# Sixteen eight-row transfers of V in place of output weights on sixteen partitions, in a two-layer decode block

## The chip, the cores and the metric

The kernel runs on one core of one Trainium2 chip. The metric is the device time of one execution in microseconds (us). Before the change three runs took 2570.63, 2570.76 and 2570.87 us; the median is 2570.76 us. One execution was profiled; its span, from the first to the last instruction, is 2568.7 us.

## What is computed

Two tokens (batch 2, one position each, width 512) go twice through the same pair of layers: grouped-query attention over a cache of 32768 positions (32 query heads, 8 key/value heads, head size 128) and a gated feed-forward of width 1792. All is float32.

```python
def _A_ref(x, k_cache, v_cache, wq, wo):
    ...
    scores = jnp.einsum("bhqd,bhkd->bhqk", q, k) * (Dh ** -0.5)
    p = _softmax(scores, axis=-1)
    o = jnp.einsum("bhqk,bhkd->bhqd", p, v)
    return ... @ wo
def _B_ref(x, w_gate, w_up, w_down):
    ...
    h = _gelu(g) * u
    return jnp.einsum("bsf,fd->bsd", h, w_down)
x = x + _A_ref(_layernorm(x, axis=-1), ...)
x = x + _B_ref(_layernorm(x, axis=-1), ...)
x = x + _A_ref(_layernorm(x, axis=-1), ...)
x = x + _B_ref(_layernorm(x, axis=-1), ...)
```

Both attention layers read the same caches, so K and V of 16 pairs (key/value head, batch row) are read twice, 16 MB each for K and for V of a pair.

## The kernel before, in words

**Memory.** One tile `mem` of 128 partitions and 109 units takes all that comes from HBM; a unit is 512 floats (2 KB) in each partition. K or V of a pair has 64 units and normally comes as two pieces of 32 units (`CHUNK`), which is 8 MB a transfer. `take` (L150) finds a place for a piece: one of three spots of 32 units, or a fitting hole in what is left. `give` and `done` return a place when the last matmul that reads it has been written into the program.

**The stream.** `add` (L224) lists every transfer in the order in which it is to come: for each layer the query weights `wq`, then for each pair K and V, with the output weights `wo` of its head ahead of V's second piece, then gate/up (`gu`) and down (`wd`) weights. Layer 2 goes through the pairs backwards and still finds one pair's K and V of layer 1 in memory. `pump` (L183) issues the transfers in this order, each as soon as a place is free; all are issued by SyncE (SP), in order, on one queue. A transfer into a place that was used before waits in SP for the matmuls that read it and for the transfer that filled it.

**Completion semaphores.** Every transfer that a queue issues signals its landing on a semaphore. The built program has eight of them for transfers (DMAHW0 to DMAHW7), given out in turn. A transfer that gets a semaphore which an earlier transfer still holds has a wait for that earlier transfer's landing in front of it, unless SP has already waited for it.

**The work of a pair.** `scores` (L396) multiplies K's units with the queries on TensorE (PE) into the PSUM banks `S` (L414), VectorE (DVE) takes the maxima, `softmax` (L445) makes the weights, `values` (L473) multiplies V's units into the bank `A` (L485), and `combine` (L490) turns the result into `oT`. After the second batch row of a head `project` (L523) multiplies `oT` of its four query heads with the head's `wo` and adds into the bank `W`, which collects the layer's output. PE, DVE and ScalarE wait for the transfers; the program is written out by hand in this order (a manual schedule).

**Output weights on sixteen partitions.** For two of the sixteen (layer, head) combinations, head 6 in layer 1 and head 1 in layer 2 (`NARROW`, L63), part of the head's `wo` (2 and 3 of its four query heads) comes in another layout, `won`: 16 partitions instead of 128, as four transfers of four rows each (L193 to L197), in a whole spot of 32 units; the rest of that head's `wo` comes on 128 partitions as elsewhere. `narrow` (L505) then selects the matching rows of `oT` with eight small matmuls (L511), copies them (L514) and does 32 or 48 matmuls with 16 rows (L519) in place of 2 or 3 with 128 rows (L529).

Of the kernel before, what the change touches and what calls it, by code (L numbers as in the profile page):

```python
# [16 lines left out]
P = 128  # L17
NB = 2
HKV = 8
REP = 4  # L20
DM = 512
# [6 lines left out]
HALF = 2048  # L28
UNIT = 512
# [6 lines left out]
CHUNK = 32  # L36
# [23 lines left out]
WO_GROUPS = [[(0, 1), (2, 3), (4, 5), (6,), (7,)], [(7,), (6,), (5, 4), (3, 2), (1,), (0,)]]  # L60


NARROW = {(0, HKV - 2): 2, (1, 1): 3}  # L63
NROW = 16
NSEL = P // NROW


def pieces(split):

    out, s = [], 0  # L70
    for n in split:
        out.append((s, n))
        s += n
    return out
# [13 lines left out]
def plan():  # L88


    last, before = ORDER[-1], ORDER[-2]
    out = {}

    def put(kind, l, pair, spots):
        for (s, n), o in zip(parts(kind, l, pair), spots):
            out[kind, l, *pair, s] = o

    put("k", 0, before, [32, 0])
    put("v", 0, before, [64, 32])
    put("k", 0, last, [0, SPARE, 64])  # L100
    put("v", 0, last, [32, 16, 8, 4, 0])
    out["wo", 0, HKV - 1] = out["wo", 1, HKV - 1] = 105
    for i in range(8):
        out["gu", 0, i] = [94, 97.5, 101, 105][i % 4]
    for i in range(9):
        out["wd", 0, i] = out["wq", 1, i] = [94, 97, 101, 105][i % 4]
    put("k", 1, last, [96, 101, 105, 94, 64, 68, 72])
    put("k", 1, before, [85, 92, 64, 72, 32])
    put("v", 1, before, [0, 64])
    return out  # L110
# [22 lines left out]


@with_exitstack
def block_kernel(ctx: ExitStack, tc: tile.TileContext, x, consts, kt, vt, wq, wo, won, gu, wd, out):
    nc = tc.nc
    cp = ctx.enter_context(tc.tile_pool(name="cp", bufs=1))
    wk = ctx.enter_context(tc.tile_pool(name="wk", bufs=2))
# [4 lines left out]
    mem = cp.tile([P, UNITS * UNIT], F32, name="mem")  # L144
# [3 lines left out]
    planned = plan()  # L148

    def take(key, n):  # L150
        if key in planned:
            o = planned[key]
            if not any(s <= o and o + n <= e for s, e in holes):
                return None
        elif n == CHUNK:
            spots = [o for o in range(0, UNITS - CHUNK + 1, CHUNK)
                     if any(s <= o and o + n <= e for s, e in holes)]
            if not spots:
                return None
            o = spots[0]  # L160
        else:
            fit = [(e - s, -s, e) for s, e in holes if e - s >= n]
            if not fit:
                return None
            size, s, e = min(fit)
            o = -s
        for i, (s, e) in enumerate(holes):
            if s <= o and o + n <= e:
                holes[i:i + 1] = [(x, y) for x, y in ((s, o), (o + n, e)) if y > x]
                return o  # L170
        return None

    def give(o, n):
        holes.append((o, o + n))
        holes.sort()
        i = 0
        while i + 1 < len(holes):
            if holes[i][1] == holes[i + 1][0]:
                holes[i:i + 2] = [(holes[i][0], holes[i + 1][1])]
            else:  # L180
                i += 1

    def pump():  # L183
        while stream:
            key, src, rows, cols = stream[0]
            n = CHUNK if rows == NROW else cols / UNIT if key in planned else -(-cols // UNIT)
            o = take(key, n)
            if o is None:
                return
            stream.popleft()  # L190
            c = int(o * UNIT)
            at[key] = (o, n), mem[:rows, c:c + cols]
            if rows == NROW:  # L193


                for i in range(4):
                    nc.sync.dma_start(mem[i:NROW:4, c:c + cols], src[i])  # L197
            else:
                nc.sync.dma_start(at[key][1], src)

    def flat_of(key):
        if key not in at:
            pump()
        return at[key][1]

    def get(key, a):
        return flat_of(key).rearrange("p (a c) -> p a c", a=int(a))

    def done(key, s=0, n=None):

        o, size = at[key][0]
        n = size if n is None else n
        if s + n == size:
            del at[key]
        give(o + s, n)
        pump()
# [7 lines left out]
    def add(key, src, rows, cols):  # L224
        stream.append((key, src, rows, cols))
# [8 lines left out]
    for l in range(2):  # L234
        for i, (s, m) in enumerate(pieces(WQ_SPLIT[l])):
            add(("wq", l, i), wq[:, s * DM:(s + m) * DM], P, m * DM)
        for n, (g, b) in enumerate(orders[l]):
            second = meets(l, n)[1]
            vp = parts("v", l, (g, b))
            for s, m in parts("k", l, (g, b)):  # L240
                add(("k", l, g, b, s), flat(kt, g, b, s, m), P, m * UNIT)
            for s, m in [] if second else vp:
                if n % 2 == 1 and s == vp[1][0] and not meets(l, n)[0]:
                    group = wo_group(l, g)
                    o = g % 2 * HALF
                    if (l, g) in NARROW:
                        h = NARROW[l, g]
                        add(("won", l, g), won[l, :, :, :h * NSEL * DM], NROW, h * NSEL * DM)
                        add(("wo", l, g), wo[g // 2, :, o + h * DM:o + HALF], P, (REP - h) * DM)
                    elif len(group) == 2 and g == group[0]:  # L250
                        add(("wo", l, g), wo[g // 2], P, 2 * HALF)
                    elif len(group) == 1:
                        add(("wo", l, g), wo[g // 2, :, o:o + HALF], P, HALF)
                add(("v", l, g, b, s), flat(vt, g, b, s, m), P, m * UNIT)
            if meets(l, n)[0]:

                add(("wo", l, g), wo[g // 2, :, g % 2 * HALF:(g % 2 + 1) * HALF], P, HALF)
        for e in range(2):
            half_of = gu[e * P * FH:(e + 1) * P * FH].rearrange("(p c) -> p c", p=P)
            for j, (c, m) in enumerate(pieces(GU_SPLIT[l])):  # L260
                add(("gu", l, len(GU_SPLIT[l]) * e + j), half_of[:, c:c + m], P, m)
        for j, (o, m) in enumerate(pieces(WD_SPLIT[l])):
            add(("wd", l, j), wd[:, o * DM:(o + m) * DM], P, m * DM)
# [18 lines left out]
    ident = cst[:, C_ID:C_ID + P]  # L282
# [5 lines left out]
    rows = ident.rearrange("p (c r) -> p c r", r=32)[:, :, :NB]  # L288
# [31 lines left out]
    W = ps.tile([P, 512], F32, name="W")  # L320
# [5 lines left out]
    def big():  # L326
        return wk.tile([P, 512], F32, name="big")[:, :]
# [9 lines left out]
    def small():  # L337

        u = 0 if state["full"] else state["next"]
        state["next"] = 1 - u  # L340
        return M[u]
# [160 lines left out]
        diag = bass.AP(tensor=mt.tensor, offset=mt.offset, ap=[mt.ap[0], [1, REP], [P + REP, 4], [32, 4]])  # L502
        nc.vector.tensor_reduce(oT[:, :, b], diag, axis=AX.XY, op=OP.add)  # L503

    def narrow(l, g, oT, final):  # L505

        m = small()
        heads = NARROW[l, g]
        n = heads * NB
        for j in range(NSEL):  # L510
            nc.tensor.matmul(m[:NROW, n * j:n * j + n], ident[:, NROW * j:NROW * j + NROW],  # L511
                             oT[:, :heads, :].rearrange("p t b -> p (t b)"), start=True, stop=True)
        on = big()[:NROW, :NSEL * n]
        nc.vector.tensor_copy(on, m[:NROW, :NSEL * n])  # L514
        w = get(("won", l, g), NSEL * heads)
        for i in range(NSEL * heads):
            q = i % 4
            j, t = i % NSEL, i // NSEL
            nc.tensor.matmul(W[32 * q:32 * q + NB, :], on[:, n * j + NB * t:n * j + NB * t + NB], w[:, i, :],  # L519
                             start=False, stop=(final and q < heads and i + 4 >= NSEL * heads))  # L520
        done(("won", l, g))

    def project(l, g, oT, first, final):  # L523
        if (l, g) in NARROW:
            narrow(l, g, oT, final)
            h = NARROW[l, g]
            w = get(("wo", l, g), REP - h)
            for t in range(h, REP):
                nc.tensor.matmul(W[32 * t:32 * t + NB, :], oT[:, t, :], w[:, t - h, :], start=False, stop=final)  # L529
            done(("wo", l, g))  # L530
            return
        group = wo_group(l, g)
        key = "wo", l, group[0]
        w = get(key, REP * len(group))
        o = REP * (g - min(group))
        for t in range(REP):
            nc.tensor.matmul(W[32 * t:32 * t + NB, :], oT[:, t, :], w[:, o + t, :], start=first, stop=final)  # L537
        if g == group[-1]:
            done(key)
# [127 lines left out]
    for l in range(2):  # L667
        queries(l)
        stage(l, 0)
        for n, (g, b) in enumerate(orders[l]):  # L670
            if n % 2 == 0:
                oT = tiny("oT")
            p, linv = softmax(*scores(l, n, g, b))
# [16 lines left out]
    assert not stream  # L690


_INS = ["x", "consts", "kt", "vt", "wq", "wo", "won", "gu", "wd"]


def groups(x):
# [50 lines left out]
```

## Time and profile before

| what | value |
|---|---|
| median of 3 runs | 2570.76 us (2570.63 to 2570.87) |
| profiled execution, span | 2568.7 us |
| read from HBM | 1103.45 MB, 430 GB/s over the span |
| busy PE / DVE / ScalarE (ACT) / GpSimd (POOL) | 54% / 6% / 3% / 0% of the span |
| transfers by SP of V and of K at full size | 60 and 59, median 48.9 and 49.0 us from issue to landing |

The page of the profile gives, engine by engine, busy time and share of the span, then the span in 40 slices with the busy share in tenths, the clock that PE was granted, the share of time in which the 16 DMA engines were busy, and the rate. A row of a timeline gives start, duration, engine, line, operation, output and inputs, how often (x), and in brackets how long the engine had been idle before it and what ended that. "SPq" is SP's queue of issues; its duration is the issue alone, not the transfer. A row that merges several issues gives the time from the first to the end of the last.

### The profile page before, as it was taken

Reading aid. Unit: us, or ns where it says so; the run is one execution under the profiler, and the core shown is the slowest. Engines: PE = TensorE matmul, PEld = TensorE weight load, DVE = VectorE, ACT = ScalarE, POOL = GpSimd, SP = SyncE. Lnnn points to the kernel's source line nnn. Section 1 sums busy time; section 2 is a strip of 40 time slices with the busy share of each in tenths; the row PEclk is TensorE's granted clock in tenths of the full one; section 3 lists DMA queues with packets and bytes.
Section 4 is the critical chain, followed back from the end, with each engine's and each line's share of the span. In section 5 each row is a group of like instructions: output and inputs, shape, how many; then the busy total and the mean of one; then the engine's idle time right before and its main releaser. Section 6 shows DMA issues by size and latency. Waiting matters only on the chain.

```text
span 2568.7 us, 20340 instructions
## 1 busy us (share of the span) xinstructions
PE 1374.8 (54%) x9526; PEld 369.8 (14%) x9526; DVE 143.6 (6%) x483; ACT 81.4 (3%) x188; POOL 2.4 (0%) x8
## 2 busy tenths in 40 slices
PE   3545555545544554564686554454555544554657
PEld 1111111111111111111121111111111111111112
DVE  0000000000000000000011000000000000000001
ACT  0000000000000000000000000000000000000000
POOL 0000000000000000000000000000000000000000
PEclk8777777777777777777798677677776777777779
DMA  9999999999999999999999999999999999999998
GB/s 425 429 434 434 428 437 431 432 433 434 429 438 428 435 433 431 434 431 432 424 410 438 429 433 434 430 433 435 431 434 432 431 435 431 433 433 430 431 432 371
DMA packets 27507, 1104.81 MB, mean 430 GB/s; under 512 B 3200, under 2 KB 3456, under 8 KB 6912
## 3 DMA queue, kind: packets, MB, share of 16 engines
q1 hardware_dynamic: 27136, 1103.44, 99.6%
q8 instruction: 74, 1.21, 0.2%
q10 hardware_dynamic: 288, 0.08, 0.0%
q14 instruction: 9, 0.07, 0.0%
HBM read 1103.45 MB, written 0.07 MB: 430 GB/s over the span
## 4 chain that ended last, share of the span: by engine, by line
DMA 69%; PE 22%; another core or an unknown queue 8%; DVE 1%; issue 0%; ACT 0%; SPq 0%; POOL 0%; ACTq 0%; DVEq 0%
DMA mem<-in_vt 41%; DMA mem<-in_kt 24%; PE A L485 11%; PE S L414 9%; DMA aux<-in_consts 2%; DMA mem<-in_gu 1%; DMA mem<-in_wq 1%; DMA mem<-in_wd 0%; PE W L537 0%; PE M L498 0%; ACT big L494 0%; PE T L460 0%; PE W L519 0%; PE W L559 0%
## 5 line engine op out<-in xcount | busy, mean ns | idle before, releaser
L414 PE MATMUL S<-mem,aux 128*32 128x512 f32 x4032 | 575.5, 734 | 527.1 <-DMA mem<-in_kt 526.7
L485 PE MATMUL A<-mem,big 128*16 128x512 f32 x4096 | 584.7, 734 | 480.8 <-DMA mem<-in_vt 480.8
L414 PEld LDWEIGHTS S<-mem,aux 128*32 128x32 f32 x4032 | 144.9, 132 | 945.3 <-issue 508.2
L485 PEld LDWEIGHTS A<-mem,big 128*16 128x16 f32 x4096 | 122.6, 113 | 913.5 <-DMA mem<-in_vt 514.9
L417 DVE TENSOR_REDUCE aux<-S 128x1 f32<-128x512 f32 x63 | 43.6, 691 | 1110.1 <-PE S L414 1110.1
L457 ACT ACTIVATE big<-S,aux 128x512 f32<-128x512 f32 x63 | 42.7, 683 | 1187.1 <-DVE aux L453 1187.1
L460 PE MATMUL T<-aux,big 128*128 128x128 f32 x256 | 50.2, 342 | 39.0 <-ACT big L457 38.7
L503 DVE TENSOR_REDUCE aux<-M 128x4 f32<-128x64 f32 x32 | 7.2, 225 | 1103.4 <-PE M L498 1103.4
L494 ACT ACTIVATE big<-A,aux 128x512 f32<-128x512 f32 (+1 forms) x34 | 22.3, 661 | 1149.0 <-PE A L485 1149.0
L461 DVE COPY big<-T 128x512 f32<-128x512 f32 x64 | 43.8, 691 | 59.8 <-PE T L460 59.8
L460 PEld LDWEIGHTS T<-aux,big 128*128 128x128 f32 x256 | 35.8, 172 | 49.7 <-ACT big L457 49.5
L498 PE MATMUL M<-aux,big 128*128 128x128 f32 x128 | 21.3, 287 | 24.9 <-ACT big L494 24.9
L465 PE MATMUL M<-aux 128*128 128x4 f32 x64 | 17.2, 339 | 29.4 <-DVE aux L463 29.4
L449 PE MATMUL M<-aux 128*128 128x128 f32 x32 | 10.3, 323 | 34.5 <-DVE aux L447 34.5
L373 PE MATMUL M<-mem,aux 128*32 128x512 f32 x128 | 20.6, 690 | 4.4 <-DMA mem<-in_wq 3.9
L498 PEld LDWEIGHTS M<-aux,big 128*128 128x128 f32 x128 | 13.4, 140 | 53.2 <-ACT big L494 53.2
L465 PEld LDWEIGHTS M<-aux 128*128 128x128 f32 x64 | 14.4, 280 | 39.1 <-DVE aux L463 39.1
L537 PE MATMUL W<-mem,aux 128*2 128x512 f32 x96 | 12.5, 592 | 3.8 <-DVE aux L503 3.8
L333 PE MATMUL A<-aux 128*128 128x256 f32 (+2 forms) x42 | 14.3, 421 | 0.3 <-DVE aux L350 0.3
L449 PEld LDWEIGHTS M<-aux 128*128 128x128 f32 x32 | 4.2, 133 | 63.6 <-DVE aux L447 63.6
L359 PE MATMUL M<-aux 128*128 128x8 f32 x2 | 0.6, 356 | 23.2 <-DMA aux<-in_x 23.2
L457 ACT ACTIVATION_READ_ACCUMULATOR big<-S,aux 128x1 f32 x63 | 12.3, 196 | 0.0
(102 smaller groups left out, 188.8 us busy)
## 6 DMA issues: line engine op xcount, KB each, us to landing
mem<-in_gu SPq DMA_DIRECT2D x16, 896.0 KB, 24.5
mem<-in_wo SPq DMA_DIRECT2D x5, 2048.0 KB, 53.5
mem<-in_vt SPq DMA_DIRECT2D x2, 4096.0 KB, 42.2
mem<-in_kt SPq DMA_DIRECT2D x1, 7168.0 KB
mem<-in_wq SPq DMA_DIRECT2D x6, 1024.0 KB, 8.2
mem<-in_kt SPq DMA_DIRECT2D x1, 6144.0 KB
mem<-in_kt SPq DMA_DIRECT2D x5, 1024.0 KB, 8.7
mem<-in_kt SPq DMA_DIRECT2D x1, 4352.0 KB
```

The source lines that it names most:

```text
L333: nc.tensor.matmul(bank, ident[:, :bank.shape[0]], part.to_broadcast([P, n]), start=True, stop=True)
L373: nc.tensor.matmul(qp[32 * t:32 * t + 32, :], window(k, v), w[:, i - s, :], start=(i < 4), stop=(i >= 8 * KC - 4))
L414: nc.tensor.matmul(banks[u][32 * t:32 * t + 32, :], pad[:, PAD_Q - 4 * c:PAD_Q + 32 - 4 * c], w[:, j - s, :], start=(j == tile_of[0]), sto ...
L417: nc.vector.tensor_reduce(mx[:, u:u + 1], banks[u], axis=AX.X, op=OP.max)
L449: nc.tensor.transpose(m[:, :P], nm.to_broadcast([P, P]), ident)
L457: nc.scalar.activation(p[u], banks[u], AF.Exp, bias=bias, scale=SCALE, accum_out=ls[:, u:u + 1])
L460: nc.tensor.transpose(T[u][:, k * P:(k + 1) * P], p[u][:, k * P:(k + 1) * P], ident)
L461: nc.vector.tensor_copy(p[u], T[u])
L465: nc.tensor.matmul(m[:, :REP], both.to_broadcast([P, P]), same, start=True, stop=True)
L485: nc.tensor.matmul(A[32 * t:32 * t + 16, :], p[u][:, at_p:at_p + 16], w[:, QUAD * i + t, :], start=(j == 0), stop=(j == NU // QUAD - 1))
L494: nc.scalar.activation(md[:, i:i + 512 // n], A[:, i:i + 512 // n], AF.Copy, scale=linv)
L498: nc.tensor.transpose(m[:, c * P:(c + 1) * P], md[:, c * P:(c + 1) * P], ident)
```

## The change

No output weights come on 16 partitions any more: `NARROW`, `narrow` and the array `won` go, and the two heads project like all others, with `wo` of 4 units on 128 partitions (`wo_group` has them as groups of one). Instead two of V's pieces, the second piece of head 6, row 1, in layer 1, and the second piece of head 1, row 0, in layer 2, are split by units: the first 26 units come as one transfer of 128 rows, the last 6 units as sixteen transfers of eight rows each (12 KB a row, 96 KB a transfer). Transfer `i` takes rows `r, r+4, ... r+28` with `r = 32*(i//4) + i%4`.

```diff
-NARROW = {(0, HKV - 2): 2, (1, 1): 3}
-NROW = 16
-NSEL = P // NROW
+ASIDE = 6
+ASIDE_OF = {("v", 0, HKV - 2, 1, CHUNK), ("v", 1, 1, 0, CHUNK)}
...
-            n = CHUNK if rows == NROW else cols / UNIT if key in planned else -(-cols // UNIT)
+            n = cols / UNIT if key in planned else -(-cols // UNIT)
...
-            if rows == NROW:
-                for i in range(4):
-                    nc.sync.dma_start(mem[i:NROW:4, c:c + cols], src[i])
+            if key in ASIDE_OF:
+                m = cols - ASIDE * UNIT
+                nc.sync.dma_start(mem[:, c:c + m], src[:, :m])
+                for i in range(P // 8):
+                    r = 32 * (i // 4) + i % 4
+                    nc.sync.dma_start(mem[r:r + 29:4, c + m:c + cols], src[r:r + 29:4, m:])
...
-                    if (l, g) in NARROW:
-                        h = NARROW[l, g]
-                        add(("won", l, g), won[l, :, :, :h * NSEL * DM], NROW, h * NSEL * DM)
-                        add(("wo", l, g), wo[g // 2, :, o + h * DM:o + HALF], P, (REP - h) * DM)
-                    elif len(group) == 2 and g == group[0]:
+                    if len(group) == 2 and g == group[0]:
...
-    def narrow(l, g, oT, final):
-        m = small()
...
     def project(l, g, oT, first, final):
-        if (l, g) in NARROW:
-            narrow(l, g, oT, final)
...
-            return
         group = wo_group(l, g)
```

More of the change, by code (lines that the diff above doesn't have):

```diff
@@ L135, in block_kernel @@
 @with_exitstack
-def block_kernel(ctx: ExitStack, tc: tile.TileContext, x, consts, kt, vt, wq, wo, won, gu, wd, out):
+def block_kernel(ctx: ExitStack, tc: tile.TileContext, x, consts, kt, vt, wq, wo, gu, wd, out):
     nc = tc.nc
@@ L503, in combine @@
         nc.vector.tensor_reduce(oT[:, :, b], diag, axis=AX.XY, op=OP.add)
-    def narrow(l, g, oT, final):
-        m = small()
[L508 to L521, printed above, removed]
-    def project(l, g, oT, first, final):
-        if (l, g) in NARROW:
-            narrow(l, g, oT, final)
[L526 to L530, printed above, removed]
-            return
+    def project(l, g, oT, first, final):
         group = wo_group(l, g)
@@ L690, in block_kernel @@
     assert not stream
-_INS = ["x", "consts", "kt", "vt", "wq", "wo", "won", "gu", "wd"]
+_INS = ["x", "consts", "kt", "vt", "wq", "wo", "gu", "wd"]
 def groups(x):
@@ L730 @@
         "wo": f(np.asarray(A_wo).reshape(HKV // 2, 2 * REP, P, DM).transpose(0, 2, 1, 3)).reshape(HKV // 2, P, 2 * HALF),
-        "won": f(np.asarray(A_wo).reshape(HKV, REP, NSEL, 4, 4, DM)[[g for _, g in NARROW]]
-                 .transpose(0, 4, 3, 1, 2, 5)).reshape(len(NARROW), 4, 4, REP * NSEL * DM),
         "gu": halves(np.asarray(B_w_gate), np.asarray(B_w_up)),
```

## The prediction

> **What bounds the kernel now.** I read the page first: the busy shares, the DMA row of the 40 slices, the chain that ended last and the costliest groups.
>
> ```profile
> PE 1374.8 (54%) x9526; PEld 369.8 (14%) x9526; DVE 143.6 (6%) x483; ACT 81.4 (3%) x188; POOL 2.4 (0%) x8
> DMA  9999999999999999999999999999999999999998
> DMA 69%; PE 22%; another core or an unknown queue 8%; DVE 1%; issue 0%; ACT 0%; SPq 0%; POOL 0%; ACTq 0%; DVEq 0%
> L485 PE MATMUL A<-mem,big 128*16 128x512 f32 x4096 | 584.7, 734 | 480.8 <-DMA mem<-in_vt 480.8
> ```
>
> The DMA engines are busy in every slice, PE a little over half the time, and PE's idle time before V's matmuls was ended by V's transfers in all 480.8 us. A table by stages (length, then busy time per engine, granted clock, DMA share, GB/s) says it for the stages of the change (1090 to 1140 and 2330 to 2430) and for the layers' border:
>
> ```profile
> 20.00:1030.00 1010.00, 518.55 (x3511) 138.26 (x3511) 52.38 (x176) 29.01 (x66) 0.55 (x1) 0.73 1.00 432
> 1090.00:1140.00 50.00, 28.94 (x208) 7.54 (x201) 3.26 (x12) 2.13 (x5) 0.00 (x0) 0.74 1.01 434
> 1280.00:1340.00 60.00, 47.16 (x376) 15.74 (x380) 6.19 (x29) 4.82 (x12) 1.10 (x2) 1.00 0.99 409
> 2330.00:2430.00 100.00, 58.51 (x417) 14.57 (x417) 5.70 (x17) 2.73 (x6) 0.00 (x0) 0.74 1.00 432
> ```
>
> So the time is the bytes over 432 GB/s, as long as the stream never runs dry; an idle microsecond of the whole stream is a microsecond of the kernel, and no stage has slack to give it back (0.99 even at the border). The bytes are the same after the change. What it can alter is how they lie on the 16 engines, and whether SP issues in time.
>
> **How many transfers SP may have in flight.** The timeline of SP's queue, its waits and line 199's summary at the end of the kernel, where the transfers are small:
>
> ```profile
> 2529.31 10.22 SPq L199 DMA_DIRECT2D mem<-in_gu  x4
> 2541.37 9.02 SPq L199 DMA_DIRECT2D mem<-in_wd  x5
> SPq L199 <- DMA mem<-in_gu: 9.0, 5, 1.8
> DMA to landing us min/median/max: 15.2/17.2/20.7
> 2554.45 1.06 PE L638 MATMUL A<-mem,aux 128*32 128x512 f32 x8 [0.23 <-DMA mem<-in_gu]
> 2556.63 1.06 PE L638 MATMUL A<-mem,aux 128*32 128x512 f32 x8 [0.70 <-DMA mem<-in_gu]
> ```
>
> Transfers of `gu` land 2.18 us apart (2556.63 less 2554.45), and one takes 17.2 us from issue to landing: 17.2/2.18 = 7.9. Eight are in flight, and SP's issues wait for landings of `gu`. That is the eight completion semaphores: the ninth issue waits for the first to land. With 8 MB pieces this binds nobody, since memory holds only three. The built order of the changed kernel on SP, with the semaphores that each issue waits for, shows where it binds (layer 1, shortened; layer 2 is alike; I name the sixteen transfers a0 to a15):
>
> ```
> mem<-in_kt 128x16384 [DMAHW0, PE]    k of head 6, row 1, second piece
> mem<-in_vt 128x16384 [DMAHW1, PE]    v, first piece
> mem<-in_wo 128x2048
> mem<-in_vt 128x13312 [DMAHW2, PE]    v, second piece, 26 units
> mem<-in_vt 8x3072 [PE], then x3      a0 to a3
> mem<-in_vt 8x3072 [DMAHW3]           a4 waits for k's second piece
> mem<-in_vt 8x3072 [DMAHW4]           a5 waits for v's first piece
> mem<-in_vt 8x3072 [DMAHW5]           a6 waits for wo
> mem<-in_vt 8x3072 [DMAHW6]           a7 waits for the 26 units
> mem<-in_vt 8x3072 [DMAHW7, 0 to 6]   a8 to a15 wait for a0 to a7
> mem<-in_kt 128x16384 [DMAHW7, PE]    next k waits for a8
> ```
>
> a7 can't be issued before the 26 units have landed on every engine. By then nothing is queued but a0 to a6, which half of the engines carry; behind a7 on SP stand eight more issues and then all later K and V. **The stream runs dry**, once a layer.
>
> **The price, step by step.** Rows of SP and PE around the place in layer 1, SP's and PE's in layer 2, and the group of the `won` issues (min/median/max ns):
>
> ```profile
> 1075.91 2.62 SPq L197 DMA_DIRECT2D mem<-in_won  x4
> 1078.58 0.44 SPq L199 DMA_DIRECT2D mem<-in_wo  x1
> 1097.53 0.33 SPq L199 DMA_DIRECT2D mem<-in_vt  x1
> 2328.22 2.49 SPq L197 DMA_DIRECT2D mem<-in_won  x4
> L197 SPq DMA_DIRECT2D mem<-in_won x4: 576/588/724, 1075.9 to 1078.0; - x4
> 1107.92 9.45 PE L485 MATMUL A<-mem,big 128*16 128x512 f32 x64 [5.21 <-DMA mem<-in_vt]
> 1128.87 9.21 PE L485 MATMUL A<-mem,big 128*16 128x512 f32 x64 [11.51 <-DMA mem<-in_vt]
> 1140.70 4.29 PE L519 MATMUL W<-mem,big 16*2 16x512 f32 x32 [0.27 <-DVE big L514]
> 1148.36 8.02 PE L414 MATMUL S<-mem,aux 128*32 128x512 f32 x64
> 2359.83 9.84 PE L485 MATMUL A<-mem,big 128*16 128x512 f32 x64 [4.85 <-DMA mem<-in_vt]
> 2381.62 9.18 PE L485 MATMUL A<-mem,big 128*16 128x512 f32 x64 [11.96 <-DMA mem<-in_vt]
> ```
>
> Landing of the 26 units: V's first piece is seen at 1107.92; 1 MB of `wo` and 6.5 MB of V at 432 GB/s are 2.4 + 15.8 = 18.2 us: 1126.1.
>
> Nine issues, a7 to a15: the trace has four-row issues, four in 2.49 or 2.62 us, and a 128-row one of 0.44; eight rows are not shown. I take 0.62 each, the four-row pitch (it is the nearer form): 5.6 us, so the next K is issued at 1131.7. Bounds: 0.44 each (4.0 us) and 0.78 (724 ns and a gap; 7.0 us).
>
> From that issue into an empty queue until the 8 MB are seen: the kernel's start shows the same case, its end a small one.
>
> ```profile
> 0.74 0.40 SPq L199 DMA_DIRECT2D mem<-in_wq  x1
> 1.19 0.89 SPq L199 DMA_DIRECT2D mem<-in_kt  x2
> SPq L199 <- DMA mem<-in_wq: 27.1, 9, 20.8
> 2566.16 0.35 SPq L591 DMA_DIRECT2D out<-big  x1
> SPq L741 <- DMA out<-big: 1.1, 1, 1.1
> ```
>
> 8 MB of `wq` are issued at 0.74, SP begins to wait at 1.19 + 0.89 = 2.08 and waits 20.8: seen at 22.9, 22.1 us after the issue, where the bytes are 19.4. The start costs 2.7. By the 64 KB output (0.35 + 1.1, less 0.1 for its bytes) it would be 1.4; I take 2.7, the same form.
>
> So K is seen at 1131.7 + 22.1 = 1153.8. Before: 1128.87 + 19.4 = 1148.3 (PE begins at 1148.36). Layer 1 loses **5.5 us**. Layer 2: 2359.83 + 18.2 + 5.6 + 22.1 = 2405.7 against 2381.62 + 19.4 = 2401.0: **4.7 us**. The second number is smaller because `won` was larger there and V's second piece came later.
>
> What costs nothing: eight selecting matmuls, a copy and 32 or 48 narrow matmuls (4.29 us in layer 1) leave PE, two or three matmuls per head with 128 rows return; PE idles 11.51 and 11.96 us for V at that place, so they are hidden; without that cover they would be worth some 5 and 8 us. The spot that `won` held is free, so V's second piece is issued at 1075.9 and not at 1097.53; that is about 25 us ahead of need instead of some 10 and hides nothing new. a0 to a6 (7 x 0.62) are issued while the queue is full. PE's last 12 matmuls on V wait for all sixteen transfers; its other 52 take 52/64 x 9.21 = 7.5 us from 1126.1, and a15, issued at 1131.1, should land some 2 us later: level. The queues of ACT and POOL are not passed.
>
> **Sum:** 5.5 + 4.7 = +10.2 us on the profiled execution, 2568.7 to 2578.9. The median of the runs is 2.1 above that span; I add the same to it: 2570.76 + 10.2 = **2581.0 us**. With both prices at their lower ends (each layer -1.6 and -1.3) the sum is +4.4, with the issue at its upper end +13.0.
>
> [...]
>
> ```profile
> q1 hardware_dynamic: 27136, 1103.44, 99.6%
> q8 instruction: 74, 1.21, 0.2%
> ```
>
> 187 full transfers and the output at 16 x (8 + 1) packets and eight `won` transfers at 4 x 2 make 27072 + 64 = 27136: four rows took four engines. [...]
>
> **The rivals.** *The issues stay ahead, and the engines come level* (not slower). If SP passes all sixteen issues before the 26 units land, only the distribution counts. [...] Engines without sixteenths are spared 12 KB in each of 8 rows, 96 KB or 3.6 us a layer at 432/16 = 27 GB/s. Before, they were spared 2 and 3 query heads of `wo`, 2 KB in each of 8 rows: 32 and 48 KB, 1.2 and 1.8 us. Gain 7.2 - 3.0 = 4.2 us: 2566.6. It decides if at least seventeen transfers may be in flight; the 7.9 above speaks against it. 5 in 100.
>
> *The same, but a partition's way into memory is the limit and not the engine.* Then rows moved to other engines load what they loaded before, and the 3.0 us that `won` spared are lost: 2573.8. No row here tells way from engine. 3 in 100. [...]
>
> *Layer 1's loss is given back at the layers' border.* Then 4.7 remain: 2575.5. For it: the rate is only 409 GB/s there; against it: a DMA share of 0.99. 6 in 100.
>
> *The sixteenths come one after the other*, each of the nine issued when the one before has landed: 9 x (1.5 + 0.5) = 18 instead of 5.6 us, twice 12.4 more: 2605.8. The built order speaks against it (a8 waits for a0, long landed). 6 in 100; a third of that, three such waits a layer, is 2589.
>
> **How the numbers follow.** My forecast, the dry stream, has 80 in 100. The range holds it with its bounds (2575.2 to 2583.8) and reaches up to the three waits and down to the border's case: 2575.0 to 2589.0. About 0.2% (5.1 us) is what a measurement here can tell from no change. The first two rivals lie within it, the third half: faster 0.02 (a larger gain than 4.2), same 0.11, slower 0.87.
>
> **What would show it.** Right: SP issues a7 only when PE begins V's second piece, nine issues some 0.6 us apart follow, the next K's matmuls begin near 1153.8 with idle time ended by its transfer, the slices' rate dips in two places. Wrong: SP's issues of a7 to a15 long before V is used; K's matmuls at 1148; a DMA share of 1.00 in both stages. The lower bounds hold if the gap between V and K shrinks to 2 or 3 us.

## The result, and the profile after

| | before | after |
|---|---|---|
| median | 2570.67 us (2570.59 to 2570.87, 5 runs) | 2585.2 us (2584.92 to 2585.96, 5 runs) |
| profiled execution, span | 2568.7 us | 2583.8 us |
| granted clock, mean | 0.746 | 0.748 |

The ratio is 1.0057, with a 95% interval of 1.0045 to 1.0069: the changed kernel is 14.5 us slower. The forecast was slower by 10.2, 2581.0 us in a range of 2575 to 2589. The span grew by 15.1 us.

From the page of after: the DMA engines' busy share and the rate in the 40 slices, the queue of SP's transfers (packets, MB, share of the engines' time) and the chain that ended last:

```profile
DMA  9999999999999999989999999999999999998999
GB/s 423 437 429 431 434 436 429 436 431 431 437 434 430 432 436 432 431 375 436 422 414 439 429 432 436 431 433 434 431 433 435 432 429 437 435 430 383 424 426 385
q1 hardware_dynamic: 27584, 1103.44, 99.2%
DMA 72%; PE 20%; another core or an unknown queue 6%; DVE 1%; SPq 1%; issue 0%; ACT 0%; POOL 0%; ACTq 0%; DVEq 0%
```

The DMA engines' row, nines up to the last slice before, has two eights inside, and the rate drops to 375 and 383 GB/s in the same slices, the 18th and the 37th: the two places of the change. SP's queue now has 1% of the chain. The same bytes (1103.44 MB) went as 27584 packets, 512 more than the 27072 that the prediction counts for full transfers: 32 transfers, each with 8 packets for its rows and 8 for the completion, so every sixteenth lay on eight engines. Followed from the end of one packet to the start of the next, the trace has seven packets of 12 KB in a row on each of eight engines in layer 1, a0 to a6, and none of these on the other eight. The table by stages puts numbers to it; the columns are those of the prediction's table:

```profile
1090.00:1140.00 50.00, 31.73 (x203) 8.46 (x195) 3.29 (x12) 2.14 (x5) 0.00 (x0) 0.75 0.87 363
2330.00:2430.00 100.00, 48.20 (x355) 12.63 (x347) 4.65 (x14) 2.73 (x6) 0.00 (x0) 0.76 0.92 390
1280.00:1340.00 60.00, 47.97 (x372) 15.43 (x364) 5.73 (x26) 4.13 (x11) 1.10 (x2) 0.97 1.01 411
```

The share of busy DMA engines fell from 1.01 to 0.87 in 50 us and from 1.00 to 0.92 in 100 us: 7.0 and 8.0 us of a standing stream, together close to the 15.1 us by which the span grew. At the layers' border (1280 to 1340) the stream is full in both kernels. The timelines of SP's queue and of PE, of after, in layer 1 and in layer 2:

```profile
1077.87 0.33 SPq L195 DMA_DIRECT2D mem<-in_vt  x1
1078.77 53.62 SPq L198 DMA_DIRECT2D mem<-in_vt  x16
1132.50 0.85 SPq L200 DMA_DIRECT2D mem<-in_kt  x2
...
2338.07 53.47 SPq L198 DMA_DIRECT2D mem<-in_vt  x16
2391.63 0.86 SPq L200 DMA_DIRECT2D mem<-in_kt  x2
```

```profile
1107.93 8.86 PE L482 MATMUL A<-mem,big 128*16 128x512 f32 x64 [3.37 <-DMA mem<-in_vt]
1126.45 8.97 PE L482 MATMUL A<-mem,big 128*16 128x512 f32 x52 [9.67 <-DMA mem<-in_vt]
1136.36 1.90 PE L482 MATMUL A<-mem,big 128*16 128x512 f32 x12 [0.95 <-DMA mem<-in_vt]
1155.72 8.87 PE L411 MATMUL S<-mem,aux 128*32 128x512 f32 x64 [13.33 <-DMA mem<-in_kt]
...
2367.02 9.07 PE L482 MATMUL A<-mem,big 128*16 128x512 f32 x64 [5.41 <-DMA mem<-in_vt]
2385.25 7.62 PE L482 MATMUL A<-mem,big 128*16 128x512 f32 x52 [9.16 <-DMA mem<-in_vt]
2394.48 1.90 PE L482 MATMUL A<-mem,big 128*16 128x512 f32 x12 [1.61 <-DMA mem<-in_vt]
2415.92 8.53 PE L411 MATMUL S<-mem,aux 128*32 128x512 f32 x64 [15.41 <-DMA mem<-in_kt]
```

Sixteen issues, some 11 us of work, take 53.6, and the next K's issue comes behind them. SP's single issues, in the trace, show the step: a6 at 1110.38, a7 at 1126.42, just as PE sees the 26 units (1126.45), then one every 0.67 us up to a15 at 1131.77 and K at 1132.50; in layer 2 a7 at 2385.22 and K at 2391.63. K's matmuls begin at 1155.72 and 2415.92. Before, K had landed at 1148.18 and 2400.94 (the landings in the trace), and PE took it up at 1148.36 and, held until then by the narrow matmuls, at 2404.55:

```profile
2404.55 7.98 PE L414 MATMUL S<-mem,aux 128*32 128x512 f32 x64
```

The waits of SP's queue (us in total, times, longest) and the group of the new issues (min/median/max ns) name the cause:

```profile
SPq L198 <- DMA mem<-in_vt: 68.0, 4, 18.7
```

```profile
L198 SPq DMA_DIRECT2D mem<-in_vt x32: 623/624/769, 1078.8 to 2390.9; - x32
```

Four waits of the 32 issues were for V: in each layer one for the first piece and one for the 26 units. The second of them stops the stream.

### The profile page after: what moved, and what is told of

Read it like the earlier page. It is cut to its first block, busy times and chain, and to the rows that moved or that the text cites. A ratio compares the mean times of both kernels' runs of the same rounds, so it can differ in the third digit from the quotient of the medians.

```text
span 2583.8 us, 20167 instructions
## 1 busy us (share of the span) xinstructions
PE 1363.5 (53%) x9424; PEld 367.6 (14%) x9424; DVE 143.5 (6%) x481; ACT 81.4 (3%) x188; POOL 2.4 (0%) x8
## 3 DMA queue, kind: packets, MB, share of 16 engines
q1 hardware_dynamic: 27584, 1103.44, 99.2%
## 4 chain that ended last, share of the span: by engine, by line
DMA 72%; PE 20%; another core or an unknown queue 6%; DVE 1%; SPq 1%; issue 0%; ACT 0%; POOL 0%; ACTq 0%; DVEq 0%
DMA mem<-in_vt 38%; DMA mem<-in_kt 30%; PE A L482 11%; PE S L411 8%; DMA aux<-in_consts 2%; DMA mem<-in_gu 1%; DMA mem<-in_wq 1%; SPq L198 0%; PE T L457 0%; DMA mem<-in_wd 0%; DVE big L458 0%; DVE aux L414 0%; PE W L530 0%; PE A L411 0%
## 5 line engine op out<-in xcount | busy, mean ns | idle before, releaser
L356 PE MATMUL M<-aux 128*128 128x8 f32 x2 | 0.6, 356 | 23.2 <-DMA aux<-in_x 23.2
L609 PE MATMUL A<-mem,aux 128*32 128x512 f32 (+1 forms) x64 | 10.5, 635 | 4.0 <-DMA mem<-in_gu 2.8
```

## The experiments

All times below stand beside 2570.8 us for the kernel before, measured with them (2570.81, 2570.76 and 2570.82 us in the three groups). Theory: the loss is the dry stream, that is, the number of issues that stand between the landing of the 26 units and the next K. Rivals: the loss of the narrow weights, the bytes set aside and the engines that carry them, and a shared way into memory.

### What the loss hangs on: `even`, `halves`, `one_unit`

`even` sets nothing aside; the narrow weights stay gone:

```diff
-ASIDE_OF = {("v", 0, HKV - 2, 1, CHUNK), ("v", 1, 1, 0, CHUNK)}
+ASIDE_OF = set()
```

> Neither output weights on 16 partitions nor split V pieces: every transfer has 128 rows. Theory (the loss of the changed kernel is a stream that runs dry behind the semaphore waits): nothing waits, and only the bytes that the old layout spared the late engines come back, 1.2 + 1.8 us: about 2574 us, 3 above before. Rival (the loss comes from taking the narrow output weights out): near the changed kernel's 2585 us.

Measured: 2573.65 us (2573.02 to 2574.55), ratio 1.0011 (1.0002 to 1.0021). The removal alone costs 2.8 us; the other 11.6 belong to the sixteen transfers. K's matmuls in `even`, in layer 1 and in layer 2 (the account of the prediction uses them):

```profile
1149.17 9.57 PE L411 MATMUL S<-mem,aux 128*32 128x512 f32 x64 [6.19 <-DMA mem<-in_kt]
2402.40 9.30 PE L411 MATMUL S<-mem,aux 128*32 128x512 f32 x64 [6.59 <-DMA mem<-in_kt]
```

`halves` doubles the number of issues and leaves bytes and engines:

```diff
-                    nc.sync.dma_start(mem[r:r + 29:4, c + m:c + cols], src[r:r + 29:4, m:])
+                    for x in (m, m + ASIDE // 2 * UNIT):
+                        y = x + ASIDE // 2 * UNIT
+                        nc.sync.dma_start(mem[r:r + 29:4, c + x:c + y], src[r:r + 29:4, x:y])
```

> Each of the sixteen transfers is cut in two by units: 32 of three units, same rows, same bytes on the same engines. Theory: 16 more issues of 0.67 us in the dry time of each layer, 10.7 us a layer: 2585.2 + 21.4 = 2606.6 us, 2603 to 2608. Rival (bytes or distribution): 2585 us, unchanged.

Measured: 2605.62 us (2605.27 to 2606.87), ratio 1.0136 (1.0121 to 1.0151). Twice sixteen more issues cost 20.4 us, 0.64 each, in line with 0.62 to 0.67 for one issue. In layer 1 K is issued 10.5 us later than in after (1132.50) and used 10.6 us later (1155.72):

```profile
1142.98 0.85 SPq L202 DMA_DIRECT2D mem<-in_kt  x2
1166.28 9.06 PE L413 MATMUL S<-mem,aux 128*32 128x512 f32 x64 [12.69 <-DMA mem<-in_kt]
```

`one_unit` leaves the number and takes five sixths of the bytes away (`ASIDE = 1`):

> The changed kernel with one unit aside instead of six: 31 units in one transfer, then sixteen transfers of eight rows of 2 KB. If the number of transfers behind the wait sets the loss: V's first piece is seen at 1107.9, 1 MB of wo and 31/32 of 8 MB take 2.4 + 18.8 = 21.2, so the eighth sixteenth is issued at 1129.1 (changed kernel: 1126.4); nine issues take 6.1 again, the next K is issued at 1135.2 and, with almost nothing of the sixteenths ahead of it, is seen some 22.1 to 23.2 us later, at 1157.3 to 1158.4 (changed kernel 1155.7). Both layers: 3 to 5.5 us more than the changed kernel, 2588 to 2591 us. If the bytes set aside (or the engines that carry them) set it, a sixth of them costs a sixth of what separates the changed kernel from the one without sixteenths: 2573.65 + 11.5/6 = 2575.6 us.

Measured: 2591.0 us (2589.87 to 2591.72), ratio 1.0078 (1.0061 to 1.0095). Its timeline of PE and SP in layer 1:

```profile
1129.20 8.79 PE L482 MATMUL A<-mem,big 128*16 128x512 f32 x64 [12.06 <-DMA mem<-in_vt]
1135.25 0.85 SPq L200 DMA_DIRECT2D mem<-in_kt  x2
1158.87 9.32 PE L411 MATMUL S<-mem,aux 128*32 128x512 f32 x64 [16.69 <-DMA mem<-in_kt]
```

Landing at 1129.2, nine issues of together 6.05 us, K 23.6 us behind its issue. Fewer bytes aside made it slower, not faster: the 31 units ahead land 2.75 us later than the 26 did, and K's issue, nine issues behind, is 2.75 us later too. The rival with the bytes (2575.6) is out. Of the three, the count of issues behind the wait is the one that moves the time.

### Issuing earlier: `around`, `two`, `four`

If the dry spell is all there is, a kernel that issues the sixteenths without it must come near 2574 us. Three did that, and none came near.

`around` issues a0 to a4, then the 26 units, a5 to a10, the next K, and the rest:

```diff
-                nc.sync.dma_start(mem[:, c:c + m], src[:, :m])
...
-                    nc.sync.dma_start(mem[r:r + 29:4, c + m:c + cols], src[r:r + 29:4, m:])
+                    rest.append((mem[r:r + 29:4, c + m:c + cols], src[r:r + 29:4, m:]))
+                for _ in range(5):
+                    nc.sync.dma_start(*rest.popleft())
+                nc.sync.dma_start(mem[:, c:c + m], src[:, :m])
+                for _ in range(6):
+                    nc.sync.dma_start(*rest.popleft())
+                continue
...
+            while rest:
+                nc.sync.dma_start(*rest.popleft())
```

> The sixteen transfers stay, in another order on SP: five ahead of the 26 units, six behind them, then the next K piece, then the last five. No issue waits for a landing while the engines' queues are empty. Theory: the loss of 14.5 us goes; about 2567 us if an engine's load counts (before less 4.2), about 2574 us if a partition's way into memory counts. Rival (sixteen small transfers or the uneven engines cost by themselves): 2580 us or more.

Measured: 2599.05 us (2597.97 to 2599.82), ratio 1.0109 (1.0094 to 1.0124). A miss, 25 us above the expectation of the theory. Its table by stages:

```profile
1110.00:1130.00 20.00, 6.44 (x56) 1.36 (x48) 0.00 (x0) 0.00 (x0) 0.00 (x0) 0.76 1.00 380
1130.00:1150.00 20.00, 8.16 (x52) 1.67 (x52) 0.00 (x0) 0.00 (x0) 0.00 (x0) 0.67 1.05 378
1150.00:1170.00 20.00, 5.76 (x44) 1.62 (x48) 0.23 (x1) 1.28 (x2) 0.00 (x0) 0.61 0.96 335
```

Read the last two columns together: the engines are busy all the time (about 1.00), so the stream is not dry, but it moves 335 to 380 GB/s in place of 430. The single packets in the trace show where the time goes (layer 1): the forty 12 KB packets of a0 to a4, rows 0 to 63, took 0.46 us each, the forty of a11 to a15, rows 64 to 127, 0.94 in the median, and 64 KB packets of other transfers, 2.42 us elsewhere, up to 4.8.

`two` makes two transfers of the six units, by rows:

```diff
-                for i in range(P // 8):
-                    r = 32 * (i // 4) + i % 4
-                    nc.sync.dma_start(mem[r:r + 29:4, c + m:c + cols], src[r:r + 29:4, m:])
+                for r, n in ((0, 119), (119, 9)):
+                    nc.sync.dma_start(mem[r:r + n, c + m:c + cols], src[r:r + n, m:])
```

> The six units come as two transfers, 119 and 9 rows, instead of sixteen; 119 rows should lie on seven engines, 17 rows each. No semaphore is short. Theory: no dry stream, so below 2577 us; 2567 us if engine load counts, about 2574 us if the way into memory counts (the 119 rows then share ways with other engines). Rival (uneven engines cost by themselves): 2580 us or more.

Measured: 2613.1 us (2612.28 to 2613.97), ratio 1.0164 (1.0147 to 1.018), a miss, with a busy but slower stream again:

```profile
1110.00:1130.00 20.00, 7.98 (x56) 1.54 (x48) 0.00 (x0) 0.00 (x0) 0.00 (x0) 0.67 1.04 318
1130.00:1150.00 20.00, 8.55 (x52) 1.71 (x52) 0.00 (x0) 0.00 (x0) 0.00 (x0) 0.67 0.97 223
```

The page tells on how many engines the rows lay:

```profile
q1 hardware_dynamic: 27360, 1103.44, 99.2%
```

`even` has 27072. By the counts above each transfer gives one packet per row and one completion packet per engine (a sixteenth 8 + 8); 119 + 9 rows on seven and nine engines would add 119 + 7 + 9 + 9 = 144 a layer, 288 in all, which is the difference. So the count fits 119 rows on seven engines, seventeen rows each; what it shows by itself is sixteen engines for the two transfers together. This kernel was badly chosen and tells only that.

`four` keeps the row order of memory and takes 32 rows a transfer:

```diff
-                for i in range(P // 8):
-                    r = 32 * (i // 4) + i % 4
-                    nc.sync.dma_start(mem[r:r + 29:4, c + m:c + cols], src[r:r + 29:4, m:])
+                for r in range(0, P, 32):
+                    nc.sync.dma_start(mem[r:r + 32, c + m:c + cols], src[r:r + 32, m:].rearrange("(j i) c -> j i c", i=4))
```

> The six units as four transfers of 32 rows in place of sixteen of eight; source and destination row by row as before, the source written as 8 x 4 rows, which should put four rows on each of eight engines. Then 4 + 1 transfers need no wait for a completion semaphore, and SP is never late. If the stream's dry spell were the only thing that costs, this kernel is within 2 us of the one without sixteenths, 2572 to 2576 us. If two engines that write the same 64 rows' places hinder each other, as the run with the reordered issues suggests (12 KB packets of rows 64 to 127 took 0.93 us and not 0.46, and 64 KB packets up to 4.8 us and not 2.42), it comes near that run: 2592 to 2602 us, with the rate at 330 to 390 GB/s for some 40 us in each of the two places and no idle engines. Should the four transfers use sixteen engines, two rows each, the packets show it.

Measured: 2592.12 us (2591.11 to 2594.55), ratio 1.0083 (1.0068 to 1.0099). No issue waits, and the stream is slow without being dry; SP's timeline and the table by stages:

```profile
1078.81 1.73 SPq L197 DMA_DIRECT2D mem<-in_vt  x4
```

```profile
1110.00:1130.00 20.00, 6.82 (x56) 1.41 (x48) 0.00 (x0) 0.00 (x0) 0.00 (x0) 0.76 1.01 312
1130.00:1150.00 20.00, 11.36 (x92) 2.92 (x92) 0.23 (x1) 1.28 (x2) 0.00 (x0) 0.84 1.00 348
```

Its page shows that the eight engines of the expectation did not come about:

```profile
q1 hardware_dynamic: 27456, 1103.44, 99.6%
```

384 more than `even`: 2 x 4 x (32 + 16), so 32 rows lay on sixteen engines, two rows each. Why the source written as 8 x 4 rows did not make it eight, no run shows.

### Whose way: the extra loads

To take the dry spell and the order out of it, the next kernels load all of V as one transfer and then load a part of it once more into free memory that nobody reads. `again_low` does it with 32-row transfers of six units and rows 0 to 63, `again_high` with rows 64 to 127 (`range(64, 64 + 64, 32)`):

```diff
+            nc.sync.dma_start(at[key][1], src)
             if key in ASIDE_OF:
...
+                o = take(("again",), ASIDE)
+                d = int(o * UNIT)
+                for r in range(0, 0 + 64, 32):
+                    nc.sync.dma_start(mem[r:r + 32, d:d + ASIDE * UNIT],
+                                      src[r:r + 32, cols - ASIDE * UNIT:].rearrange("(j i) c -> j i c", i=4))
+                give(o, ASIDE)
```

> All of V as one transfer, no sixteenths; instead the six units of rows 0 to 63 are loaded a second time into a free place that nobody reads, as two transfers of 32 rows (8 x 4), right behind V's second piece in both layers: 768 KB more at each place, 8 packets of 12 KB on each of eight engines. At 0.46 us a packet these engines are 3.7 us later at each place; if they carry what they carry for the same rows anyway, that is all: between 2573.7 (taken up by the engines that are early) and 2573.65 + 7.4 = 2581 us, best estimate 2577. Rival, that any extra small packets slow the whole stream: 2590 or more, like the run with the reordered issues. The pair with the rows 64 to 127 tells whose rows matter.

> As the run before it, but with rows 64 to 127 loaded a second time: the same bytes, transfers, engines and places in the order. If a partition's way into memory is what engines share, these packets meet the engines that carry rows 64 to 127 in every full transfer: 12 KB packets take 0.93 us, 64 KB packets grow, and the time is well above the run with rows 0 to 63, 2588 to 2602 us. If only bytes on engines count, both runs agree within 2 us (2574 to 2581).

Measured: 2589.47 us (2589.31 to 2589.87) and 2590.32 (2588.42 to 2590.84), ratios 1.0072 (1.0057 to 1.0087) and 1.0074 (1.0059 to 1.0089). Equal, and 16 us above `even` for 1.5 MB, whose bytes are worth 3.6. As they stand these runs spoke against the shared way; but their packets (27264, 2 x 2 x (32 + 16) more than `even`) lay on sixteen engines and not on the eight that both expectations count with, so the two did not test what they were made for. The pair was made again with eight-row transfers of eight units, 512 KB at each place, r from 0 to 3 in `again_own` and from 64 to 67 in `again_other`, beside the same bytes as one 128-row transfer of two units (`again_full`):

```diff
-ASIDE = 6
+ASIDE = 8
...
+                for r in range(0, 0 + 4):
+                    nc.sync.dma_start(mem[r:r + 29:4, d:d + ASIDE * UNIT], src[r:r + 29:4, cols - ASIDE * UNIT:])
```

> [...] Here the extra load is four transfers of eight rows: rows r, r+4, ... r+28 for r = 0 to 3, eight units (16 KB a row), 512 KB at each of the two places, again into a free place that nobody reads. [...] If a shared way into memory is what slows the stream, nothing is slow here: 64 KB packets stay at 2.42 us, eight engines are 4 x 0.6 = 2.4 us later at each place, and the time is 2573.65 + (0 to 4.8) = 2574 to 2578.5 us. If small packets or strided sources slow the stream, it equals the next run, 2581 to 2587 us.

> [...] If the way into memory is shared: the 768 KB of the pair before cost 15.8 to 16.7 us, so 512 KB cost some 10.5 to 11: 2584 us (2581 to 2587), with 64 KB packets of 3 to 5 us and a rate below 400 GB/s for some 20 us. If only bytes and engines count: as the run before, 2574 to 2578.5.

> The same 512 KB at each place as one transfer of two units in all 128 rows: the price of the bytes alone. 512 KB at 432 GB/s are 1.2 us: 2573.65 + 2.4 = 2576 us (2575 to 2577.5) by every theory.

Measured: `again_own` 2576.89 us (2576.56 to 2578.1), ratio 1.0024 (1.0015 to 1.0033); `again_other` 2589.43 (2588.85 to 2590.18), 1.0073 (1.0058 to 1.0088); `again_full` 2576.26 (2575.66 to 2576.61), 1.0021 (1.0011 to 1.003). The first and the last lie within what was expected; `again_other` is 2.4 us above the upper end of its range. The tables by stages of `again_own` and of `again_other`:

```profile
1110.00:1130.00 20.00, 8.02 (x60) 1.62 (x56) 0.00 (x0) 0.00 (x0) 0.00 (x0) 0.67 0.99 427
1130.00:1150.00 20.00, 11.41 (x92) 2.69 (x92) 0.22 (x1) 1.28 (x2) 0.00 (x0) 0.76 1.02 440
```

```profile
1110.00:1130.00 20.00, 7.00 (x56) 1.41 (x48) 0.00 (x0) 0.00 (x0) 0.00 (x0) 0.76 1.00 351
1130.00:1150.00 20.00, 12.09 (x92) 2.88 (x92) 0.23 (x1) 1.28 (x2) 0.00 (x0) 0.76 1.00 375
```

The number of engines (27200 packets in both, eight engines a transfer), the sizes and the place in the order are the same; only the row numbers differ by 64. Rows 0 to 31 cost about their bytes, like the full transfer (3.2 and 2.6 us over `even`, 2.4 by the bytes). Rows 64 to 95 cost 12.5 us more, 6.3 a place: at a DMA share of 1.00 in both stages 76 and 65 GB/s are missing for 20 us each, 2.8 MB, 6.5 us at 434. The 32 extra packets of 16 KB in layer 1 have a median of 0.61 us in the one and of 1.27 in the other. Packets of 64 KB over 2.6 us between 1090 and 1200: 3 and 67. So what slows the packets goes with the row number and not with their size or number. The source rows in HBM change along with the rows in memory, so these runs do not tell on which side it arises, and that packets share a way into memory is the author's explanation, which no run shows. Nor does the size follow from two packets that share one time: in layer 1 of `again_other` the extra packets took 18 us too long in sum, the 64 KB packets 85, where sharing in pairs would give 18 for these too. In `around` 64 KB packets were slowed as well, up to 4.8 us in place of 2.42. Why so many are slowed stays open.

## Why the prediction was right, and where its sizes were off

**The mechanism held, term by term.** Only eight transfers in flight, a7 waiting for the 26 units, nine issues and K behind them, a restart from an empty queue: each is in the rows of after (and in its trace SP's 220 issues name eight semaphores in turn, 27 or 28 issues each). `halves` moved the time by the count of issues, and `one_unit` shows that fewer bytes aside don't shorten it.

| term, layer 1 / layer 2 | predicted | measured |
|---|---|---|
| 26 units seen | 1126.1 / 18.2 after V's first piece | 1126.4 / 18.2 after it |
| from there to K's issue | 5.6 / 5.6 | 6.1 / 6.4 |
| K's issue to K seen | 22.1 / 22.1 | 23.2 / 24.3 |
| loss of the layer | 5.5 / 4.7 | 7.4 / 7.7 |

The measured losses are 1155.72 less 1148.36, and 2415.92 less 2401.0 (before, K had landed there at 2400.94) less the 7.2 us by which V's first piece was late already (2367.02 less 2359.83).

**The mis-sized terms.** The step "nine issues, 0.62 each" had the issue right (624 ns) and left out the 0.05 us between two: 0.5 and 0.8 us. The larger part is "K is seen 22.1 later", taken from the kernel's start: 1.1 and 2.2 us. The packets of the queues between K's issue and its landing, in after and at the kernel's start before (0 to 23 us), hold one thing that the start has not:

```profile
q1 hardware_dynamic: 225, 10.63, 101.3%
q8 instruction: 1, 0.02, 0.2%
```

```profile
q1 hardware_dynamic: 160, 9.44, 97.9%
q10 hardware_dynamic: 144, 0.00, 0.4%
```

An instruction fetch of 16 KB (q8) runs on one engine during K's transfer, in each of the two layers. It takes 0.92 us in layer 1, and the 64 KB packet behind it 2.92 in place of 2.42. The trace does not name engines, but where one packet ends and the next one starts they can be followed (these figures are worked out in this way, and no run was made without a fetch):

- In `one_unit`, where only 2 KB packets stand ahead of K, the engine with the fetch ends K's piece 1.5 and 0.8 us behind the next one, and K is seen 23.6 and 23.0 us after its issue. Without that engine it would be some 22.1 and 22.2, the price of the prediction.
- In layer 1 of after the engine with the fetch is the last as well, at 1155.22, but only 0.5 us behind the next, which began K at 1135.07 behind a sixteenth (engines without one began from 1133.58 on). So about 0.5 of the 1.1 us are the fetch; the rest goes with the last sixteenths, which stand ahead of K on some engines.
- In layer 2 of after the fetch is not what ends last: its engine is through at 2415.13, while two engines that began K 1.7 us after the other fourteen end at 2415.36 and 2415.52. What held these two is open.

In all of these K is seen when its last engine ends (1155.72 behind 1155.22 and 2415.92 behind 2415.52), however early the others are.

**A term that the sum left out.** The prediction prices the lost narrow weights at 3.0 us, but among the rivals only; its sum has nothing for them, and `even` measured 2.8. Against `even` the two dry places cost 6.6 us (1155.72 less 1149.17) and 7.5 (2415.92 less 2402.40, less the 6.0 by which V's first piece was late, 2367.02 less 2360.99). That is 14.0, while the spans differ by 12.4 (2583.8 less 2571.4): some 1.6 us come back, 0.5 between the two places and 1.1 behind the second. So it is in part chance that the two losses in the table add up to just the 15.1 us of the span. Whether what comes back is the levelling of the engines that the first rival has, or only that K was seen when its last engine ended, no run tells.

**What cost nothing** cost nothing: PE's last 12 matmuls followed the 52 with 0.95 and 1.61 us of idle time, well inside the 13.33 and 15.41 us that PE waits for K. (By the prediction's own rows V's second piece is issued 32 us ahead of need, 1107.9 less 1075.9, and not about 25; it changes no term.)

**The rivals.** *Given back at the border*: refuted, 1.01 busy there and the loss of layer 1 still there at 2367. *One after the other*: refuted, one issue each 0.67 us. *Issues ahead, engines level* (2566.6) and *the same with the way into memory as the limit* (2573.8) had the wrong condition here. `around` and `four` come nearest to it, with no issue that waits while the queues are empty, and both prices were far off: 2599.05 and 2592.12 us. The first rival's gain of 4.2 us takes the engines without sixteenths for the late ones. No run shows that it is so throughout; in the trace of after, layer 1, six of the eight engines with a0 to a6 are through with the 26 units at 1119.1 to 1121.5, the other two at 1125.3 and 1125.4, and six of the eight without them at 1123.8 to 1126.0, the other two at 1119.0 and 1119.8. The second rival has the way into memory as the limit, which no run shows either; `again_own` and `again_other` show a price that goes with the row number (2576.89 and 2589.43 us), and the rival took from its limit only that nothing is gained by spreading. That an extra transfer's rows slow the stream was in none of my numbers. And the dry spell shielded the change: a8 to a15, the rows 64 to 127, met little of a running stream. The 12 KB packets of layer 1 have a median of 0.47 us in after and of 0.91 in `four`, and after (2585.2) is faster than `four` (2592.1), where nothing waits. That the sum came out right thus hangs on the dry spell itself: it has no term for packets that are slowed, and in a full stream one would have been needed.

No version here beats the kernel before. `even` is the best without narrow weights, 2.8 us above it.

## What to carry to other kernels

Before a transfer is cut into many, count what may be in flight on its queue: here the ninth issue waited for a landing (a7, until 1126.42 and 2385.22), and the price was not its own bytes but all that was queued behind it, an empty stream and a restart, 7.4 and 7.7 us. The rows of an extra transfer beside a full stream were not free to choose: 1 MB of rows 0 to 31 cost 3.2 us, 1 MB of rows 64 to 95 15.8. And a DMA share of 1.00 was not full speed (380 GB/s in `around`, 432 before); read it beside the rate.

## What the runs showed of the hardware that was not expected

- A 16 KB packet took 0.61 us (median) into rows 0 to 31 and 1.27 us into rows 64 to 95 beside a full stream; 512 KB of the latter cost 6.3 us more.
- The engines counted as busy while packets were slowed: 223 GB/s at a DMA share of 0.97 in `two` (1130 to 1150).
- A transfer of 32 rows ran on sixteen engines, two rows each (27456 packets in `four`), although its source was grouped by four rows; 119 and 9 rows ran on sixteen engines together (27360 packets in `two`).
- Starting from an empty queue, the first 64 KB packet of each engine took 3.1 us (median) at the kernel's start and 2.9 and 3.0 in the middle of after, and not 2.42, and the earliest began 1.0 to 1.1 us after the issue.
- An issue on SP took 0.33 to 0.44 us for 128 rows (after), a median of 0.42 for 32 rows (`four`) and of 0.62 for eight (after).
